# Residual transfers issued from ScalarE instead of SP, with new list rules, in a threshold-attention and MLP-mixer kernel

## Chip, cores and metric

The kernel runs on one core of one Trainium2 chip. The metric is the device time of one execution in microseconds (us). All data is float32.

## The reference

What is computed, cut to the core (8 images, 8 heads, 576 tokens, head width 64; 512 features, 256 token units, 1536 channel units):

```python
scores = scale * np.matmul(q, k.transpose(0, 1, 3, 2))
thresh = np.max(scores, axis=-1, keepdims=True) - tau
scores = np.where(scores >= thresh, scores, -1000000000.0)
attn = np.exp(scores - np.max(scores, axis=-1, keepdims=True))
attn = attn / (np.sum(attn, axis=-1, keepdims=True) + 1e-09)
x = np.matmul(attn, v)          # heads side by side: (8, 576, 512)
h = np.maximum(x.transpose(0, 2, 1) @ w_tok1, 0.0) @ w_tok2
u = x + h.transpose(0, 2, 1)
out = u + np.maximum(u @ w_ch1, 0.0) @ w_ch2
```

## The kernel before

One image is a *row* of the plan, b = 0 to 7. The attention of a row is cut into units of 128 queries by two heads' keys; two units make a *round*. A round is: scores on TensorE (L839), row maxima on VectorE (`mx`, L856), the bias on GpSimd (L862), masking (L872) and exponentials (L882) on ScalarE, the inverse sums on VectorE (L276, L277), scaling on GpSimd (L285). For b > 0 the probabilities are turned in blocks of 32 by 32 on VectorE (`turn_blocks`, tile `T`, L315) and brought to their places by four transfers a unit (`move`, tile `eT`, L327). Three units make a group of the values product (L365, L370), which fills `xT` (L374). The loads of q, k (L106) and v (L120) for later pairs of heads go out all along; `split_middle` (L341) prepares part of v on VectorE.

Beside the attention of row b runs the mixer of row b - 1: the token layers (L454, L472; their inputs are partly brought by `x_sb` transfers, L406 and L412) and, for 256 of a row's tokens, the channel layers in `make_groups`: `ch1` (L962) with a relu (`relu` on ScalarE, L967, or `relu_v` on VectorE, L970), and `ch2` (L980). The rest of the rows is put off (`spill`, L531) and done after the last attention by the class `Late`, on TensorE nearly alone.

The residual of a group: `turn_u` (L947) turns `u` on VectorE into the tile `us`, `move_u` (L954) moves it by eight transfers of 64 KB into the tile `ut`, `leave` (L994) adds `ut` to the product of `ch2` and writes the sum to `us`, and `store` (L1004) sends `us` to the output in two transfers. There is one buffer of `us` and one of `ut`, so the next group's turn waits for the stores and adds of the last group. This is done for b = 1 to 6, one group each: 48 transfers of `move_u` and 12 stores. Row 0 has two groups without `turn_u`. `Late` has its own turn and transfers (L1316, L1321), which the change leaves alone.

Each engine executes its instructions in the order in which they were listed. That order is made while the kernel is built, by the class `Scheduler`: every step is an `Op` with an engine, an estimated duration, the steps that it waits for and a rank. The scheduler keeps a clock for each engine (`pe`, `act`, `dve`, `pool`, `sp`), takes the step that can start first, and among those that can start at once the one of lowest rank. Steps that only issue transfers name them as `dmas=(count, KB, issue)`: so many issues of so many us on their queue, then the bytes at `RATE` and `LANDING` us until a step that waits for them may start. Some steps may go to either of two engines (`other`): the scheduler takes the one that can start first. Products that leave a PSUM bank use one of two banks during the attention (`banked`); the bank is free again when ScalarE or VectorE has emptied it. The scores have six banks of their own, for one round. The lines that decide a start:

```python
        def start(self, x, eng):
            t = max([d.landed or d.end + (d.lag if d.eng != eng else 0.0) for d in x.deps] + [0.0])
            if x.dmas and len(self.in_flight) == FLIGHT:
                t = max(t, self.in_flight[0])
```

While the planner's TensorE clock is under `WARM_UNTIL` = 110 us, idle time of TensorE is filled with turns of a unit matrix (`warm`).

Of the kernel before, what the change touches and what calls it, by code (L numbers as in the profile page):

```python
# [21 lines left out]
def kernel(  # L22
# [25 lines left out]
    nc = tc.nc  # L48
# [10 lines left out]
    NP = H // 2  # L59
# [486 lines left out]

    TOKEN_RANK, TOKEN_AFTER_TOKEN = 1.5, 2.5
    SLACK, SPARE = 1.0, 4.0
    FLIGHT, RATE, LANDING = 8, 214.0, 1.5
    WARM_UNTIL, WARM_GAP, WARM_TURN = 110.0, 0.6, 0.11  # L550

    class Op:
# [15 lines left out]
    class Scheduler:  # L568
# [42 lines left out]
            return t  # L611

        def start(self, x, eng):
            t = max([d.landed or d.end + (d.lag if d.eng != eng else 0.0) for d in x.deps] + [0.0])
            if x.dmas and len(self.in_flight) == FLIGHT:
                t = max(t, self.in_flight[0])
            if x.shared and eng == "dve":
                t = max(t, self.clock["pool"])
            if x.bank:
                frees = [b.free for b in self.banks if b.free is not None]  # L620
                if not frees:
                    return None
                t = max(t, min(frees))
            return max(t, self.clock[eng])
# [95 lines left out]
    sched = Scheduler()  # L720
# [3 lines left out]
    def key_op(*key):  # L724
        return keyed.get(key)

    def put(key, x):
        keyed[key] = x
        return x
# [59 lines left out]
    def make_pair(n):  # L789
        b, p = pairs[n]  # L790
        if n:
            ahead = (key_op("prep", n - 2, 0), key_op("prep", n - 2, 1))
            for lo in range(0, LOADS, 2):
                put(
                    ("load", n, lo),
                    sched.op(
                        "sp",
                        0.9,
                        lambda lo=lo: load_qk(n, (nc.sync,) * 2, range(lo, lo + 2)),
                        ahead,  # L800
                        1 if n >= NP else 0,
                        after=(key_op("load", n - 1, LOADS - 2),),
                        dmas=(2, 107, 0.58),
                    ),
                )
            slot = last_round(n - 2) if n > 1 else -1
            for which in (1, 0):
                put(
                    ("prep", n, which),
                    sched.op(  # L810
                        "dve",
                        PREP,
                        lambda which=which: prep(n, ((which, 0, S // 32),)),
                        [key_op("load", n, lo) for lo in range(0, LOADS, 2)] + [key_op("S", slot)],
                        3,
                        after=(key_op("prep", n - 1, 0),),
                    ),
                )
        free = key_op("V", last_values(n - 4)) if n >= VL else None
        if n > 1:  # L820
            put(("loadv", n), sched.op("sp", 2.0, lambda: load_v(n), (free,), 0, after=(key_op("loadv", n - 1),), dmas=(4, 70, 0.67) if n >= NP else (1, 280, 0.5)))
        put(("split", n), sched.op("dve" if n >= NP else "pool", 0.25 if n >= NP else 0.5, lambda: split_middle(n), (key_op("loadv", n), free), 2))


# [92 lines left out]
    state = {"ch2": [], "stores": [], "adds": []}  # L917
    early = {}

    def make_early(b):  # L920

        turn_main, turn_rest, move_main, move_rest = early_x(b)
        have = [key_op("X", rank_of_group(b, 0, g)) for g in range(3)]
        free = early.get(b - 1, converted)
        turns = [sched.op("dve", 1.1, lambda c=c: turn_main(c), have + free, 2) for c in range(HQ)]
        before = [x for k, x in keyed.items() if k[0] == "tok" and k[1] == b - 1 and len(k) == 3 and x.first_layer]
        moved = [sched.op("sp", 1.2, lambda i=i: move_main(i), turns + before, 0, dmas=(1, 131, 0.645)) for i in range(4)]
        last = sched.op("dve", 0.35, turn_rest, moved, 2)
        moved += [sched.op("sp", 0.6, lambda i=i: move_rest(i), [last] + before, 0, dmas=(1, 16, 0.6)) for i in range(4)]
        early[b] = moved  # L930
        xreads.setdefault(b, []).extend(turns + [last])

    def make_groups(b, halves):
        uT = xTs[b]
        reads = []
        for i in range(NOW[b]):
            s = {}
            n, nt = GR, GR // P
# [10 lines left out]
                        in_=uT[:, :, GR * i + P * m : GR * i + P * m + P].rearrange("q c (r a) -> q c a r", a=4),  # L949
                    )  # L950

            def move_u(k, s=s):
                for m in range(nt):
                    nc.sync.dma_start(  # L954
                        out=s["ut"][:, m, k, :], in_=s["us"][32 * k : 32 * k + 32, m]
                    )

# [48 lines left out]
            have = halves["20"] + (halves["21"] if i else [])  # L1006
            moved = []
            if b:
                turn = sched.op("dve", 1.2, turn_u, have + state["stores"] + state["adds"] + (converted if b == 1 else []), 5)
                reads.append(turn)  # L1010
                moved = [sched.op("sp", 1.2, lambda k=k, m=move_u: m(k), (turn,), 1, dmas=(nt, 53, 0.645)) for k in range(4)]
            relus = []
            for j in range(NJ):
                x, y = sched.banked(
# [14 lines left out]
            for t in range(nt):  # L1029
                outs = []  # L1030
                for c in range(0, NCC, wide):
                    make = sched.banked_in_two if b else sched.banked
                    x, y = make(
                        2.6 if b else 2.8,
                        lambda bank, *half, t=t, c=c, f=ch2: f(bank, t, c, *half),
                        "dve" if b else "act",
                        0.35 if b else 0.21,
                        lambda bank, t=t, c=c, f=leave: f(bank, t, c),
                        relus + moved + (converted if not b else []) + (state["stores"] if not b else []),
                        2,  # L1040
                        b,
                        1 if b else 0,
                    )
                    outs.append(y)
                    seconds.append(x)
                    if not b:
                        reads.append(x)
                    fills[b] = fills.get(b, 0.0) + x.cost * wide
                adds += outs
                stores.append(sched.op("sp", 0.35, lambda t=t, f=store: f(t), outs, 2, dmas=(1, 150, 0.35)))  # L1050
            state["ch2"], state["stores"], state["adds"] = seconds, stores, adds
        return reads

# [52 lines left out]
    def make_round(it):  # L1106
# [28 lines left out]
        for u in us:  # L1135
            b, p0, t = units[u]
            s = sched.op("pool", 1.46, lambda u=u: scale(u), (n,), 1)
            deps = [s]
            G = rank_of_group(b, p0, t // GU)
            if not b:  # L1140
                deps += [key_op("V", G - 2) if t % GU == 0 else None, key_op("T", u - 1)]
                for third in range(3):
                    x, y = sched.banked(
                        0.33,
                        lambda bank, u=u, third=third: turn(u, third, bank),
                        "act",
                        0.4,
                        lambda bank, u=u, third=third: turned(u, third, bank, nc.scalar.copy),
                        deps,
                        0,  # L1150
                        other=("dve", 0.5, lambda bank, u=u, third=third: turned(u, third, bank, nc.vector.tensor_copy)),
                    )
                    put(("turned", u, third), y)
                    deps = [x]
                put(("T", u), x)
                if t % GU == GU - 1:
                    make_group(b, p0, t // GU)
                    if t // GU == 2 and p0:
                        rows_due.append(b)
                continue  # L1160
            deps += [key_op("T", u - 1), key_op("M", u - 3)]
            put(("T", u), sched.op("dve", 1.31, lambda u=u: turn_blocks(u), deps, 4))
            put(
                ("M", u),
                sched.op(
                    "sp",
                    2.4,
                    lambda u=u: move(u),
                    (key_op("T", u), key_op("V", G - 2) if t % GU == 0 else None),
                    0,  # L1170
                    after=(key_op("M", u - 1),),
                    dmas=(4, 147, 0.645),
                ),
            )
            if t % GU == GU - 1:
                make_group(b, p0, t // GU)
                if t // GU == 2:
                    (rows_due if p0 == NP - 2 else early_due).append(b)
# [326 lines left out]
```

## Time and profile before

| | |
|---|---|
| three runs | 1259.86, 1265.16, 1265.19 us; median 1265.16 |
| profiled execution, its own time | 1261.13 us |
| its span, first to last instruction | 1259.4 us |
| busy: TensorE / VectorE / ScalarE / GpSimd | 1228.2 / 751.7 / 565.3 / 316.1 us |
| issues of `eT`, q and k loads, `ut`, v loads on SP | 504, 250, 128, 112 |

In the profile's lines PE is TensorE's matmuls, PEld its weight loads, DVE VectorE, ACT ScalarE, POOL GpSimd, SP the sync engine; a q behind the name (SPq) means the instruction queue, which issues a transfer or waits. `out<-in` are the program's tile names. "L315" is a line of the kernel. An arrow names who ended a wait. The share of the clock that TensorE was granted is 1.00 in nearly all of the span. A table by stretches gives for each its length, then busy time and number of instructions of PE, PEld, DVE, ACT and POOL, then granted clock, busy share of the transfer engines and GB/s. The mixed part, attention beside the mixer, lasts until about 892 us; what follows is `Late`.

### The profile page before, as it was taken

What the parts mean: (1) busy time and instruction counts of PE and PEld (TensorE: products, weight loads), DVE (VectorE), ACT (ScalarE), POOL (GpSimd) and SP (SyncE); (2) the same over time, 40 slices, a digit from 0 to 9 for tenths busy, and PEclk for the clock granted to TensorE, in tenths of its full rate; (3) what the DMA queues carried; (4) which work ended last, traced back from release to release, by engine and by line L of the source; (5) the groups of instructions that cost most, each with busy time, mean ns of one, the idle gap of its engine ahead of it and who ended that gap; (6) DMA issues with size and microseconds to landing.
All of it is one profiled execution on the core that took longest, in us unless ns stands there. A gap on an engine that the chain in (4) does not pass through costs nothing.

```text
span 1259.4 us, 20636 instructions
## 1 busy us (share of the span) xinstructions
PE 1228.2 (98%) x7590; PEld 989.2 (79%) x7590; DVE 751.7 (60%) x1136; ACT 565.3 (45%) x1236; POOL 316.1 (25%) x518
## 2 busy tenths in 40 slices
PE   9898999999999999999999999999999999999998
PEld 8566788797677777777777777688888888888887
DVE  6799972657667667666856766762443534444443
ACT  6998853554645664654565556530110202011120
POOL 4666641232223333233223332310001010000000
PEclk9999999999999999999999999999999999999999
DMA  9655985356777687676766866550201101021011
GB/s 165 149 135 165 242 195 118 89 121 169 163 168 161 160 169 154 171 158 151 190 145 144 191 154 153 131 152 22 59 19 65 34 26 43 17 67 26 26 34 34
DMA packets 324212, 149.17 MB, mean 118 GB/s; under 512 B 223696, under 2 KB 316880, under 8 KB 324112
## 3 DMA queue, kind: packets, MB, share of 16 engines
q1 hardware_dynamic: 322240, 147.64, 51.1%
q8 instruction: 60, 0.98, 0.3%
q10 hardware_dynamic: 1872, 0.21, 0.1%
q14 instruction: 40, 0.33, 0.1%
HBM read 47.32 MB, written 13.50 MB: 48 GB/s over the span
## 4 chain that ended last, share of the span: by engine, by line
PE 79%; DVE 6%; SPq 4%; DMA 3%; ACT 2%; issue 1%; POOL 0%; DVEq 0%; POOLq 0%
PE bank L980 12%; PE o L1326 10%; PE bank L962 10%; PE sc L839 9%; PE bank L370 8%; PE hx L1326 6%; PE bank L472 4%; PE hz L1326 4%; PE oz L1326 4%; PE hmm L1326 4%; PE bank L454 4%; PE bank L365 2%; SPq L327 2%; DVE mx L856 2%; DMA eT<-T 1%
## 5 line engine op out<-in xcount | busy, mean ns | idle before, releaser
L285 POOL TENSOR_SCALAR e<-e,rr 128x576 f32<-128x576 f32 x288 | 213.3, 758 | 294.4 <-DVE rr L277 275.8
L872 ACT ACTIVATE e<-sc,bias 128x576 f32<-128x576 f32 x288 | 194.1, 741 | 152.2 <-POOL bias L862 148.8
L882 ACT ACTIVATE e<-e,ntau 128x576 f32<-128x576 f32 x288 | 220.5, 778 | 0.3
L856 DVE TENSOR_REDUCE mx<-sc 128x2 f32<-128x1152 f32 x144 | 188.0, 1346 | 53.9 <-PE sc L839 53.6
L315 DVE STREAM_TRANSPOSE T<-e 128x1152 f32<-128x1152 f32 x126 | 169.9, 1363 | 45.8 <-POOL e L285 25.1
L980 PE MATMUL bank<-wc,g 128*128 128x256 f32 (+1 forms) x960 | 178.2, 339 | 2.6 <-ACT g L967 2.3
L962 PE MATMUL bank<-xT,wc 128*128 128x256 f32 x768 | 178.0, 385 | 2.5 <-ACT xT L374 2.0
L980 PEld LDWEIGHTS bank<-wc,g 128*128 128x128 f32 x960 | 152.4, 191 | 26.3 <-issue 4.8
L962 PEld LDWEIGHTS bank<-xT,wc 128*128 128x128 f32 x768 | 142.5, 190 | 32.0 <-issue 6.8
L839 PE MATMUL sc<-kT,qT 64*128 64x192 f32 (+1 forms) x1920 | 165.9, 334 | 0.6 <-ACT e L872 0.5
L839 PEld LDWEIGHTS sc<-kT,qT 64*128 64x128 f32 (+1 forms) x1920 | 139.0, 177 | 30.6 <-issue 17.7
L370 PE MATMUL bank<-eT,lv 128*64 128x384 f32 (+1 forms) x1024 | 135.2, 406 | 0.0
L1409 POOL TENSOR_TENSOR us<-us,ut 128x256 f32<-128x256 f32 x27 | 22.4, 844 | 385.8 <-DVE us L1247 385.8
L370 PEld LDWEIGHTS bank<-eT,lv 128*64 128x64 f32 x1024 | 74.5, 137 | 49.7 <-issue 41.9
L862 POOL TENSOR_SCALAR bias<-mx,toff 128x2 f32<-128x2 f32 x144 | 39.2, 273 | 196.8 <-DVE mx L856 189.7
L472 PE MATMUL bank<-w,a 128*128 128x192 f32 (+1 forms) x256 | 72.9, 418 | 0.4 <-DVE xT L483 0.3
L454 PE MATMUL bank<-x_sb,w 128*128 128x256 f32 x320 | 72.6, 382 | 0.3 <-DVE eT L305 0.2
L967 ACT ACTIVATE g<-bank 128x256 f32<-128x256 f32 x72 | 27.5, 382 | 99.7 <-PE bank L962 99.5
L454 PEld LDWEIGHTS bank<-x_sb,w 128*128 128x128 f32 x320 | 60.1, 190 | 10.6 <-issue 1.1
L1374 ACT ACTIVATE ga<-hmm 128x256 f32<-128x256 f32 x30 | 11.5, 383 | 117.1 <-PE hmm L1326 117.1
L1247 DVE TENSOR_TENSOR temps<-hx,temps 128x256 f32<-128x256 f32 x60 | 25.1, 418 | 56.7 <-PE hx L1326 56.6
L882 ACT ACTIVATION_READ_ACCUMULATOR e<-e,ntau 128x1 f32 x288 | 58.5, 203 | 0.0
(133 smaller groups left out, 1517.5 us busy)
## 6 DMA issues: line engine op xcount, KB each, us to landing
eT<-T SPq DMA_DIRECT2D x504, 144.0 KB, 3.0
lk<-in_k_dram SPq DMA_DIRECT2D x126, 72.0 KB, 3.0
lq<-in_q_dram SPq DMA_DIRECT2D x124, 72.0 KB, 3.2
out_dram<-us SPq DMA_DIRECT2D x32, 256.0 KB, 2.1
ut<-us SPq DMA_DIRECT2D x128, 64.0 KB, 2.1
lv<-in_v_dram SPq DMA_DIRECT2D x112, 72.0 KB, 2.6
spare<-in_moe_w_ch_dram SPq DMA_DIRECT2D x8, 512.0 KB, 3.8
extra<-in_moe_w_ch_dram SPq DMA_DIRECT2D x8, 512.0 KB, 3.9
```

What stands on the lines that cost most here:

```text
L285: nc.gpsimd.tensor_scalar(out=eh, in0=eh, scalar1=rr[:, h : h + 1], scalar2=1.0, op0=ALU.mult, op1=ALU.mult)
L315: nc.vector.transpose(out=T.rearrange("p a (c x) -> p c a x", c=NK), in_=e.rearrange("p (c a x) -> p c a x", c=NK, a=4))
L370: nc.tensor.matmul(to[r], lhsT=lv[:, j, :], rhs=e[j], start=False, stop=(c == NI - 1), skip_group_check=True)
L454: nc.tensor.matmul(to, lhsT=w1[:, t, P * m : P * m + P], rhs=x(t), start=(t == 0), stop=(t == NT - 1), skip_group_check=len(products) > 1,)
L472: nc.tensor.matmul(bank[:, n * i : n * i + n], lhsT=hidden[b][:, m, P * c : P * c + P], rhs=w2[:, m, lo : lo + n], start=(m == 0), stop=(m ...
L839: nc.tensor.matmul(sc[h][rows, f, HT * k : HT * k + HT], lhsT=qT[r, cols], rhs=kT[r, HT * f : HT * f + HT], start=True, stop=True, skip_gr ...
L856: nc.vector.tensor_reduce(out=mx[:, h], in_=sc[h][:, :, 0 : 2 * HT].rearrange("p f (k x) -> p k f x", k=2), axis=AX.XY, op=ALU.max)
L872: nc.scalar.activation(out=eh, in_=part[h], func=AF.Prelu, bias=bias[:, h], scale=SCALE, alpha=STEEP)
L882: nc.scalar.activation(out=eh, in_=eh, func=AF.Exp, bias=ntau, accum_out=rs[:, h, 0:1])
L962: nc.tensor.matmul(bank[:, 0:n], lhsT=wc1[:, j, c, :], rhs=uT[:, c, GR * i : GR * i + n], start=(c == 0), stop=(c == NCC - 1))
L980: nc.tensor.matmul(to, lhsT=s["g"][:, j, P * t : P * t + P], rhs=wc2[:, j, P * c : P * c + wide * P], start=(j == 0 and b > 0), stop=(j == ...
L1326: nc.tensor.matmul(ps, lhsT=l, rhs=r, start=start and x == 0, stop=x == len(pairs) - 1, skip_group_check=not start)
```

## The change

Five things are altered. `move_u` issues its transfers from ScalarE's queue (`nc.scalar`), as steps of the engine `act` with rank 3, and they are reckoned at 64 KB and 0.55 us per issue. The stores of rows 1 to 6 get rank -1 (2 before), 256 KB and 0.6 us. The turn of the residual is reckoned at 2.05 us (1.2 before). The issues of q and k loads, v loads, `x_sb` and `eT` are reckoned at 0.62, 0.70, 0.69 and 0.69 us (0.58, 0.67, 0.645 and 0.645 before). And a VectorE step that waits for a transfer is placed as if the transfer landed `LATE` = 2.0 us later, once the planner's TensorE clock has passed `CALM` = 200 us. What each instruction computes is the same; the planner makes another order of all of them.

```diff
--- before.py
+++ after.py
@@ -546,7 +546,7 @@
 
     TOKEN_RANK, TOKEN_AFTER_TOKEN = 1.5, 2.5
     SLACK, SPARE = 1.0, 4.0
-    FLIGHT, RATE, LANDING = 8, 214.0, 1.5
+    FLIGHT, RATE, LANDING, LATE, CALM = 8, 214.0, 1.5, 2.0, 200.0
     WARM_UNTIL, WARM_GAP, WARM_TURN = 110.0, 0.6, 0.11
 
     class Op:
@@ -611,7 +611,8 @@
             return t
 
         def start(self, x, eng):
-            t = max([d.landed or d.end + (d.lag if d.eng != eng else 0.0) for d in x.deps] + [0.0])
+            late = LATE if eng == "dve" and self.clock["pe"] > CALM else 0.0
+            t = max([d.landed + late if d.landed else d.end + (d.lag if d.eng != eng else 0.0) for d in x.deps] + [0.0])
             if x.dmas and len(self.in_flight) == FLIGHT:
                 t = max(t, self.in_flight[0])
             if x.shared and eng == "dve":
@@ -800,7 +801,7 @@
                         ahead,
                         1 if n >= NP else 0,
                         after=(key_op("load", n - 1, LOADS - 2),),
-                        dmas=(2, 107, 0.58),
+                        dmas=(2, 107, 0.62),
                     ),
                 )
             slot = last_round(n - 2) if n > 1 else -1
@@ -818,7 +819,7 @@
                 )
         free = key_op("V", last_values(n - 4)) if n >= VL else None
         if n > 1:
-            put(("loadv", n), sched.op("sp", 2.0, lambda: load_v(n), (free,), 0, after=(key_op("loadv", n - 1),), dmas=(4, 70, 0.67) if n >= NP else (1, 280, 0.5)))
+            put(("loadv", n), sched.op("sp", 2.0, lambda: load_v(n), (free,), 0, after=(key_op("loadv", n - 1),), dmas=(4, 70, 0.70) if n >= NP else (1, 280, 0.5)))
         put(("split", n), sched.op("dve" if n >= NP else "pool", 0.25 if n >= NP else 0.5, lambda: split_middle(n), (key_op("loadv", n), free), 2))
 
 
@@ -924,7 +925,7 @@
         free = early.get(b - 1, converted)
         turns = [sched.op("dve", 1.1, lambda c=c: turn_main(c), have + free, 2) for c in range(HQ)]
         before = [x for k, x in keyed.items() if k[0] == "tok" and k[1] == b - 1 and len(k) == 3 and x.first_layer]
-        moved = [sched.op("sp", 1.2, lambda i=i: move_main(i), turns + before, 0, dmas=(1, 131, 0.645)) for i in range(4)]
+        moved = [sched.op("sp", 1.2, lambda i=i: move_main(i), turns + before, 0, dmas=(1, 131, 0.69)) for i in range(4)]
         last = sched.op("dve", 0.35, turn_rest, moved, 2)
         moved += [sched.op("sp", 0.6, lambda i=i: move_rest(i), [last] + before, 0, dmas=(1, 16, 0.6)) for i in range(4)]
         early[b] = moved
@@ -949,9 +950,9 @@
                         in_=uT[:, :, GR * i + P * m : GR * i + P * m + P].rearrange("q c (r a) -> q c a r", a=4),
                     )
 
-            def move_u(k, s=s):
+            def move_u(k, eng, s=s):
                 for m in range(nt):
-                    nc.sync.dma_start(
+                    eng.dma_start(
                         out=s["ut"][:, m, k, :], in_=s["us"][32 * k : 32 * k + 32, m]
                     )
 
@@ -1006,9 +1007,9 @@
             have = halves["20"] + (halves["21"] if i else [])
             moved = []
             if b:
-                turn = sched.op("dve", 1.2, turn_u, have + state["stores"] + state["adds"] + (converted if b == 1 else []), 5)
+                turn = sched.op("dve", 2.05, turn_u, have + state["stores"] + state["adds"] + (converted if b == 1 else []), 5)
                 reads.append(turn)
-                moved = [sched.op("sp", 1.2, lambda k=k, m=move_u: m(k), (turn,), 1, dmas=(nt, 53, 0.645)) for k in range(4)]
+                moved = [sched.op("act", 1.2, lambda k=k, m=move_u: m(k, nc.scalar), (turn,), 3, dmas=(nt, 64, 0.55)) for k in range(4)]
             relus = []
             for j in range(NJ):
                 x, y = sched.banked(
@@ -1047,7 +1048,7 @@
                         reads.append(x)
                     fills[b] = fills.get(b, 0.0) + x.cost * wide
                 adds += outs
-                stores.append(sched.op("sp", 0.35, lambda t=t, f=store: f(t), outs, 2, dmas=(1, 150, 0.35)))
+                stores.append(sched.op("sp", 0.35, lambda t=t, f=store: f(t), outs, -1 if b else 2, dmas=(1, 256, 0.6)))
             state["ch2"], state["stores"], state["adds"] = seconds, stores, adds
         return reads
 
@@ -1169,7 +1170,7 @@
                     (key_op("T", u), key_op("V", G - 2) if t % GU == 0 else None),
                     0,
                     after=(key_op("M", u - 1),),
-                    dmas=(4, 147, 0.645),
+                    dmas=(4, 147, 0.69),
                 ),
             )
             if t % GU == GU - 1:
```

## The prediction

> **What bounds the kernel now.** I read the page's busy line first, then the busy times by stretch, then who ended TensorE's waits, then the time line of the queues around each of those waits.
>
> ```profile
> span 1259.4 us, 20636 instructions
> PE 1228.2 (98%) x7590; PEld 989.2 (79%) x7590; DVE 751.7 (60%) x1136; ACT 565.3 (45%) x1236; POOL 316.1 (25%) x518
> ...
> 0.00:200.00 200.00, 185.60 (x1443) 142.85 (x1443) 163.89 (x266) 158.20 (x336) 105.89 (x163) 1.00 0.76 172
> 200.00:892.10 692.10, 680.21 (x4471) 528.03 (x4472) 429.27 (x581) 352.69 (x771) 187.83 (x328) 1.00 0.64 145
> 892.10:1259.40 367.30, 362.36 (x1678) 318.34 (x1676) 158.51 (x291) 54.42 (x130) 22.42 (x27) 1.00 0.14 39
> ```
>
> The first number of a stretch is its length, the second TensorE's busy time. TensorE idles 1259.4 - 1228.2 = 31.2 us in all: 14.4 in the first 200 us (weights are converted there, and the edit of the DVE rule starts only where the planner's PE clock is past 200), 11.9 between 200 and 892 us (attention beside the mixer), 4.9 at the very end. The matmuls are the same in both kernels, and the order built from the changed one has the same number of warming turns (114) and the same order from the last values product to the end. So the change can save at most the idle time; the 11.9 us are what it aims at.
>
> ```profile
> PE bank L980 <- ACT g L967: 2.3, 2, 2.1
> PE bank L365 <- DMA x_sb<-extra: 2.2, 1, 2.2
> PE bank L962 <- ACT xT L374: 2.0, 1, 2.0
> PE bank L365 <- DMA lv<-in_v_dram: 1.3, 1, 1.3
> PE bank L978 <- DVE rr L276: 0.9, 1, 0.9
> PE bank L435 <- ACT x_sb L439: 0.7, 1, 0.7
> PE bank L365 <- DVE g L970: 0.6, 1, 0.6
> ```
>
> These are TensorE's waits from 200 to 890 us: total, times, longest. They are few and each has a place. The queue of SP (the next lines: start, duration, issues) shows what stood ahead of them.
>
> ```profile
> 323.92 3.01 SPq L954 DMA_DIRECT2D ut<-us  x4
> 327.03 5.88 SPq L327 DMA_DIRECT2D eT<-T  x8
> ...
> 520.67 0.60 SPq L1004 DMA_DIRECT2D out_dram<-us  x1
> ...
> 524.06 2.12 DVE L947 STREAM_TRANSPOSE us<-xT 128x512 f32<-128x512 f32 x2 [4.81 <-DMA out_dram<-us]
> ...
> 732.22 5.33 SPq L954 DMA_DIRECT2D ut<-us  x8
> 737.60 0.58 SPq L106 DMA_DIRECT2D lq<-in_q_dram  x1
> 738.24 0.53 SPq L106 DMA_DIRECT2D lk<-in_k_dram  x1
> 738.87 5.13 SPq L327 DMA_DIRECT2D eT<-T  x8
> 744.09 2.64 SPq L120 DMA_DIRECT2D lv<-in_v_dram  x4
> ...
> 748.60 0.36 DVE L341 TENSOR_TENSOR vl<-lv,whose 128x64 int32<-128x64 int32 x2 [3.26 <-DMA lv<-in_v_dram]
> ```
>
> SP issues back to back for 12 us after 323.92 and for 24 after 732.22, so whatever stands ahead delays all that follows. At 747.3 TensorE waited 1.3 us for lv, issued behind eight residual transfers; at 335.5 it waited 2.2 us at a values product whose last eT piece was issued at 332.3, behind four (the profile credits the last landing that it saw, x_sb). At 524.06 VectorE had stood 4.81 us at the turn of the residual, because the store that frees its buffer was issued only at 520.67; the score maxima behind it came late, and TensorE lost 2.0 us at 531.7 and 0.6 at 543.5. The 2.1 us at 760.1 is a relu of ScalarE behind late softmax work, whose maxima stood on VectorE behind transposes that waited 1.69 and 2.14 us for transfers issued up to 754.3, in the same busy stretch of SP.
>
> **The change, part by part.**
> *Residual transfers, 48 issues (6 groups x 8), from SP to ScalarE.* Taken from SP: its 48 issues last 0.602 us at the median and start 0.646 us apart (5.33 us for eight): 48 x 0.646 = 31.0 us of a queue that is busy 509 us of the 692 (821 issues). Past the others of that queue, eT, lv, lq, lk and x_sb move up by 2.6 or 5.2 us behind each place where four or eight stood. That covers the 2.2 us at 335.5 (2.6 freed), the 1.3 at 747.3 (5.2 freed) and, less surely, the 2.1 at 760.1: **-5.6 us**. The transfers themselves had slack and stay hidden: in the group issued from 732.2 the first add that reads them starts at 771.4, more than 30 us later; without that cover an add would wait their 2.1 us to landing.
>
> Added to ScalarE: the same 31.0 us, on an engine busy 352.7 of 692.1 us there. ScalarE's own issue rows (0.36 to 0.58 us, the five at the start) bound one from below, SP's row from above; I take 0.646. In the built order they stand as ten blocks of four and one of eight, so 2.6 and 5.2 us, and each first waits for VectorE's two turns (2.12 us). Directly behind ten of the eleven stands a relu (L967), behind the other a masking (L872); a PSUM bank waits for each relu, and there are two. Dearest case: the block starts when a bank is full; the bank is free 2.59 + 0.38 us later, TensorE meanwhile has one product of 8 x 0.216 = 1.73 us in the other, and loses 1.24 us; the block of eight 3.8. That is 10 x 1.24 + 3.8 = 16.2 us at most. Cheapest: nothing. The nearest row is one of ScalarE's own: four exponentials in a row (4 x 0.777 = 3.1 us) block it as long, up to 54 times in this stretch, and TensorE's waits for ScalarE there, without the two explained above, are 0.7 + 0.3 + 0.2 + 0.2 = 1.4 us, or 0.03 each. Eleven more: **+0.3 us**.
>
> *Stores first (rank -1).* No instruction added; a store is issued when the adds are done and not behind eT. It frees `us`, for which the turn waits: VectorE's 7.6 us in three waits (L947), one of which cost TensorE 2.0 + 0.6: **-2.6 us**. The eT pieces that it passes lose one issue each, 0.54 us; twelve stores, hidden by the 2.6 us blocks that left the queue.
>
> *LATE = 2.0 on VectorE's waits for transfers, dearer issues (0.69, 0.70, 0.62 in place of 0.645, 0.67, 0.58), turn at 2.05.* These only alter the list. The durations are nearer to the trace: eT issues start 0.647 us apart at the median and last 0.632 in the mean against 0.602 in the median, since 25 of 440 took over 0.8 us. The counts move: 61 relus on ScalarE and 35 on VectorE against 72 and 24; 11 x 0.42 us = 4.6 us more on VectorE, which is idle 38% of the stretch. I cost these rules at nothing by themselves, hidden behind TensorE's other products.
>
> *A new order everywhere.* Every list has places where a guess was wrong. Bounds: none, or again the 8.2 us removed. I take one stall of the usual size, **+2.0 us**; the 3.7 us of small waits stay.
>
> Sum: -5.6 - 2.6 + 0.3 + 2.0 = -5.9 us. The profiled execution took 1261.13 us (span 1259.4 and 1.7 around it), so 1255.2. The median shown, 1265.16, is 4.0 above it, the fastest run at 1259.86 below it; no trace shows what the higher ones lost. A list with less on SP should suffer less from stretched issues, so I take a third of that distance: **1256.5 us**.
>
> **Rivals.**
> 1. *New stalls for old.* The waits came from a static order against transfers of varying length, and SP still carries 773 issues. Then the 8.2 us reappear elsewhere: 1261.1 + 0.3 = 1261.4 us. For it: with the old rules already the stretches from 450 to 500 and 550 to 650 us have no TensorE idle at all, so luck counts. Against: three of the five stalls stand right behind the issues that go.
> 2. *ScalarE holds the banks (the slower side).* From 0.75 us lost per block on, 11 x 0.75 = 8.2 eats the gain; at the dearest price the time is 1261.1 - 8.2 + 16.2 + 2.0 = 1271.1 us. For it: two banks only, relus behind ten blocks, and the planner reckons 0.55 us per issue where SP's row gives 0.646. Against: ScalarE is idle half the time and the planner gives these issues its last rank.
> 3. *SP gets no relief, because the two queues issue one at a time.* Then only the stores' 2.6 us are won: 1261.1 - 2.6 + 0.3 + 2.0 = 1260.8 us. Against it, from the start of the trace:
>
> ```profile
> 0.73 0.94 SPq L106 DMA_DIRECT2D lk<-in_k_dram  x2
> ...
> 0.73 1.03 ACTq L106 DMA_DIRECT2D lk<-in_k_dram  x2
> ```
>
> Two issues on each queue in the same microsecond, none longer (0.40 to 0.58 us each) than SP's median 0.60 later, when ScalarE issues nothing. [...]
> 4. *More than the named stalls.* All idle after 200 us goes: 1261.1 - 11.9 = 1249.2 us.
>
> **How the numbers follow.** Forecast 0.43; rival 1 0.25; rival 2 0.18; rival 3 0.06; rival 4 0.08. A change of 0.5% of 1265.16 is 6.3 us, about what a measurement of this kernel can tell from none. Faster by that (below 1258.8): 0.31 of the forecast, 0.08 of rival 4, 0.02 of rival 1, together 0.41. Slower (above 1271.5): 0.13 of rival 2, 0.02 each of rivals 1 and 3, 0.17. Within: 0.42. The range leaves out the far ends of rivals 2 and 4: 1248.5 to 1268; the forecast's own is 1250 to 1261.
>
> **What would show it.** In the changed profile: the residual's issues on ScalarE's queue at about 0.65 us each, eT and lv issues without the 5 us blocks ahead; TensorE's idle from 200 us to the end of the attention near 6 us; VectorE's wait for out_dram near nothing; TensorE's waits for relus (L967) not grown. The forecast is wrong if those relu waits pass 5 us, if issues on ScalarE stretch beyond 1 us beside SP's, or if TensorE's idle time there stays near 12 us with new names.

## The result and the profile after

The changed kernel takes 1253.22 us (median of 6 runs, 1250.87 to 1255.79) against 1263.95 before (6 runs, 1259.86 to 1265.19): ratio 0.992, 95% interval 0.9901 to 0.9939, or 10.7 us less. The prediction was 1256.5. The two profiled executions, at 1261.13 and 1253.89 us, lie 7.2 us apart. The other 3.5 us of the medians' distance fit the differences in TensorE's mean granted clock, which is on record for 65 runs of the kernel before: the ten at 0.998 or more take 1260.2 us at the median, the ten at 0.993 or less 1267.4. The profiled execution of before had 0.998 where those 65 have 0.995 at the median; the profile and the runs of the changed kernel have 0.997 alike. An estimate from this is 0.003 x 1260 = 3.8 us.

The page of the changed kernel:

```profile
span 1252.1 us, 20650 instructions
## 1 busy us (share of the span) xinstructions
PE 1226.1 (98%) x7590; PEld 990.5 (79%) x7590; DVE 756.4 (60%) x1147; ACT 561.0 (45%) x1225; POOL 317.1 (25%) x518
```

Busy times by stretch, changed kernel (length, then PE, PEld, DVE, ACT, POOL busy, clock, transfers):

```profile
0.00:200.00 200.00, 186.57 (x1431) 143.22 (x1432) 163.55 (x266) 158.49 (x335) 105.92 (x163) 0.98 0.76 172
200.00:885.00 685.00, 677.34 (x4485) 529.13 (x4485) 434.50 (x592) 348.06 (x760) 188.74 (x328) 1.00 0.65 147
885.00:1252.10 367.10, 362.20 (x1677) 318.19 (x1676) 158.36 (x291) 54.45 (x130) 22.45 (x27) 1.00 0.14 39
```

The stage after the attention is as long as before; the stretch from 200 us on got shorter by the 7 us. TensorE idles 685.0 - 677.3 = 7.7 us there, against 11.9. That is 4.2 of the 7.2 us. The rest lies inside what the page counts as busy: the same 7590 matmuls are busy 1226.1 us in place of 1228.2. In the kernel before, the clock explains part of it. Behind its wait at 531.7 us TensorE was granted half the clock for 3.4 us, and like products took longer (before, TensorE's time line, then the stretch in the columns of the table above):

```profile
520.19 2.22 PE L839 MATMUL sc<-kT,qT 64*128 64x192 f32 x24
522.34 1.99 PE L962 MATMUL bank<-xT,wc 128*128 128x256 f32 x8
...
531.69 2.46 PE L962 MATMUL bank<-xT,wc 128*128 128x256 f32 x8 [2.03 <-ACT xT L374]
534.07 3.39 PE L839 MATMUL sc<-kT,qT 64*128 64x192 f32 x24
...
533.10:536.50 3.40, 3.40 (x19) 2.75 (x19) 0.77 (x4) 1.46 (x5) 1.72 (x3) 0.50 0.52 109
```

The lower two took 0.47 + 1.17 = 1.6 us longer than the upper two, so the stall at 531.7 cost 3.7 us and not 2.0. The changed kernel has no such stretch after 200 us, but one of 6.8 us from 57.4 on, which is why its first row shows 0.98. Some 1.4 us of the 7.2 stay unexplained.

TensorE's waits from 200 to 890 us, changed kernel (total us, times, longest; the four longest):

```profile
PE bank L365 <- DMA lv<-in_v_dram: 3.1, 1, 3.1
PE bank L365 <- DMA lq<-in_q_dram: 1.8, 1, 1.8
PE bank L365 <- DVE xT L483: 0.9, 1, 0.9
PE bank L365 <- DMA eT<-T: 0.8, 1, 0.8
```

All the stalls that the prediction named are gone; the two longest here are new ones, at 403.9 and 454.5 us. No relu of ScalarE stands in the list any more. From the waits of all engines in the same stretch, and from the line of the residual's issues (minimum, median and maximum in ns):

```profile
DVE vl L341 <- DMA lv<-in_v_dram: 14.1, 6, 9.5
ACT g L968 <- DMA ut<-us: 11.8, 3, 5.5
DVE T L315 <- DMA eT<-T: 7.1, 5, 1.7
```

```profile
L955 ACTq DMA_DIRECT2D ut<-us x48: 550/616/1501, 291.0 to 832.3; - x48
```

VectorE's waits for lv and eT fell to half (28.6 and 15.0 before), and its 7.6 us for the stores no longer appear. ScalarE did stand behind its own issues, 11.8 us at relus and 4.9 us at a masking, and no matmul's wait in the list above is put down to it.

The longest wait, 3.1 us, comes from the move all the same. It ends when the last eT piece has landed, at 403.7 us, and SP issued these pieces late (changed kernel: a line of SP's waits, SP's time line, TensorE's):

```profile
SPq L327 <- DMA ut<-us: 5.9, 3, 3.0
...
395.86 0.50 SPq L106 DMA_DIRECT2D lk<-in_k_dram  x1
398.77 2.50 SPq L327 DMA_DIRECT2D eT<-T  x4
...
403.88 0.87 PE L365 MATMUL bank<-eT,vl 128*64 128x384 f32 x4 [3.11 <-DMA lv<-in_v_dram]
```

SP stood 2.4 us before the eT issue, until a residual transfer that ScalarE had issued at 396.0 landed at 398.7. In this trace all 1157 transfers, of SP's queue (1104) and ScalarE's (53), report their landing on the same eight semaphores, and none of the 1149 issues that use a semaphore again starts before the transfer that used it last has landed. 33 start within 0.1 us after that landing, 13 of these behind a transfer of the other queue. The eT issue is one: it starts 0.06 us after the transfer of 396.0, which had used its semaphore, has landed. So transfers issued by ScalarE still held SP. It waited 11.0 us for residual transfers in the changed kernel from 200 to 890 us, and in no line of the kernel before. With the same list and the issues on SP (the mirror below) these eT pieces are issued from 395.80 on, and TensorE waits 0.9 us there.

### The profile page after: what moved, and what is told of

It is laid out like the page before. It is cut to its first block, busy times and chain, and to the rows that moved or that the text cites. A ratio compares the mean times of both kernels' runs of the same rounds, so it can differ in the third digit from the quotient of the medians.

```text
span 1252.1 us, 20650 instructions
## 1 busy us (share of the span) xinstructions
PE 1226.1 (98%) x7590; PEld 990.5 (79%) x7590; DVE 756.4 (60%) x1147; ACT 561.0 (45%) x1225; POOL 317.1 (25%) x518
## 4 chain that ended last, share of the span: by engine, by line
PE 87%; DVE 4%; DMA 2%; SPq 1%; issue 1%; ACT 0%; POOL 0%; DVEq 0%; POOLq 0%
PE bank L963 13%; PE bank L981 13%; PE o L1327 10%; PE sc L840 10%; PE bank L370 9%; PE hx L1327 6%; PE bank L454 5%; PE bank L472 4%; PE hz L1327 4%; PE oz L1327 4%; PE hmm L1327 4%; PE bank L365 3%; DVE mx L857 1%; SPq L327 1%; DMA lq<-in_q_dram 1%
## 5 line engine op out<-in xcount | busy, mean ns | idle before, releaser
L968 ACT ACTIVATE g<-bank 128x256 f32<-128x256 f32 x61 | 23.5, 385 | 105.9 <-PE bank L963 93.7
L454 PEld LDWEIGHTS bank<-x_sb,w 128*128 128x128 f32 x320 | 59.8, 190 | 11.8 <-ACT e L883 1.4
```

Of the source, the lines that this page charges most:

```text
L454: nc.tensor.matmul(to, lhsT=w1[:, t, P * m : P * m + P], rhs=x(t), start=(t == 0), stop=(t == NT - 1), skip_group_check=len(products) > 1,)
```

## The experiments

Each was timed against runs of the kernel before on the same chip; the ratio has its 95% interval. Differences to the changed kernel compare series whose medians of the kernel before lie between 1263.95 and 1265.38 us.

| kernel | median us | before us | ratio |
|---|---|---|---|
| changed kernel | 1253.22 | 1263.95 | 0.9920 (0.9901 to 0.9939) |
| p1: before, move alone, at its place in the list | 1257.51 | 1264.42 | 0.9953 (0.9928 to 0.9977) |
| p2: changed list, without the move | 1258.98 | 1264.42 | 0.9959 (0.9942 to 0.9976) |
| changed, LATE = 0 | 1260.29 | 1264.42 | 0.9967 (0.9948 to 0.9986) |
| changed, stores as before | 1250.22 | 1264.42 | 0.9883 (0.9854 to 0.9911) |
| before, stores first alone | 1265.74 | 1264.16 | 1.0019 (1.0006 to 1.0032) |
| before, LATE alone | 1261.54 | 1264.16 | 0.9980 (0.9961 to 0.9999) |
| changed, issues on ScalarE twice | 1275.94 | 1264.16 | 1.0098 (1.0068 to 1.0127) |
| changed, stores' rank 2 | 1251.67 | 1264.16 | 0.9914 (0.9889 to 0.9938) |
| changed, issues on ScalarE halved | 1253.34 | 1265.38 | 0.9906 (0.9884 to 0.9927) |
| changed, issue durations as before | 1258.79 | 1265.38 | 0.9949 (0.9930 to 0.9968) |
| before, all list rules, no move | 1253.76 | 1265.03 | 0.9905 (0.9888 to 0.9922) |
| changed, stores as before, LATE = 3 | 1250.71 | 1265.03 | 0.9883 (0.9868 to 0.9898) |

### The queue without the list

**Only the queue, in the list of the kernel before.**

```diff
-                    nc.sync.dma_start(
+                    nc.scalar.dma_start(
                         out=s["ut"][:, m, k, :], in_=s["us"][32 * k : 32 * k + 32, m]
```

> The list of the kernel before, unchanged in order; only the 48 issues of move_u go out from ScalarE at the place where they were listed on SP. The planner knows nothing of it, so this is the queue alone. Relief of SP (the prediction's theory): the stalls at 335.5, 747.3 and 760.1 go, 5.6 us of the 1263.95 before, so about 1258 us. New list (rival: the gain came with the new order): no gain, 1262 to 1266. ScalarE holds the banks: above 1266, with TensorE waits for relus (L967) of over 3 us.

Measured 1257.5, 6.9 us less: the relief of SP is real. TensorE's waits of this kernel, 200 to 890 us:

```profile
PE bank L962 <- ACT xT L374: 2.8, 1, 2.8
PE bank L365 <- DMA x_sb<-extra: 1.1, 1, 1.1
...
PE bank L980 <- ACT g L967: 0.9, 2, 0.6
```

The order is that of before, so places can be compared. The wait for x_sb and eT near 335 us fell from 2.2 to 1.1 us, the wait for lv at 747 us is gone, the one for the relu near 760 fell from 2.1 to 0.6. That is 3.9 of the 5.6 us priced. The clock adds to it: this trace has no stretch at half the clock between 200 and 890 us, and the nine runs have a mean clock of 0.999 where the 26 of before on that chip have 0.995. The wait behind the late store stays, as it should, since no store was moved: 2.0 before, 2.8 here, with VectorE standing 5.49 us at the turn:

```profile
522.84 2.10 DVE L947 STREAM_TRANSPOSE us<-xT 128x512 f32<-128x512 f32 x2 [5.49 <-DMA out_dram<-us]
```

**The mirror: the changed list, with the issues on SP.**

```diff
-... lambda k=k, m=move_u: m(k, nc.scalar), (turn,), 3, dmas=(nt, 64, 0.55)) ...
+... lambda k=k, m=move_u: m(k, nc.sync), (turn,), 3, dmas=(nt, 64, 0.55)) ...
```

> The list of the changed kernel, unchanged in order; only the 48 issues of move_u go out from SP at their listed place, 31 us back on that queue. Relief of SP: the 5.6 us come back, about 1259 us against 1253.2. New list: stays at 1252 to 1255.

Measured 1259.0, 5.8 us more than the changed kernel. The two agree on the move's worth with one list held fixed. This list was planned for an SP that has not these issues, though, so the mirror doesn't tell what the rules are worth without the move; the kernel for that comes below.

### The list rules

**LATE undone.**

```diff
-    FLIGHT, RATE, LANDING, LATE, CALM = 8, 214.0, 1.5, 2.0, 200.0
+    FLIGHT, RATE, LANDING, LATE, CALM = 8, 214.0, 1.5, 0.0, 200.0
```

> The changed kernel with LATE = 0: the rule on VectorE's waits for transfers alone is undone, the list is made anew. The prediction costs the rule at nothing: 1253 us, within 2. If the rule carries the gain: 1257 to 1264, and VectorE waits more for eT and lv than the 7.1 and 14.1 us of the changed kernel.

Measured 1260.3: 7.1 us of the changed kernel's gain go with a rule that had been costed at nothing. A place where it shows, VectorE's time line of this kernel, then SP's:

```profile
427.23 0.42 DVE L971 TENSOR_SCALAR g<-bank 128x256 f32<-128x256 f32 x1 [1.30 <-PE bank L963]
433.67 0.36 DVE L341 TENSOR_TENSOR vl<-lv,whose 128x64 int32<-128x64 int32 x2 [6.01 <-DMA lv<-in_v_dram]
...
436.01 1.38 DVE L315 STREAM_TRANSPOSE T<-e 128x1152 f32<-128x1152 f32 x1 [1.70 <-POOL e L285]
437.31 2.58 DVE L857 TENSOR_REDUCE mx<-sc 128x2 f32<-128x1152 f32 x2
```

```profile
429.14 2.62 SPq L120 DMA_DIRECT2D lv<-in_v_dram  x4
```

VectorE came to `vl` at 427.7 and did nothing until 433.7, when lv, issued from 429.1 on, had landed. Transposes and maxima queued behind it, and TensorE stood still for 4.3 us at 440.7, waiting for eT.

**The issue durations undone.**

```diff
-                        dmas=(2, 107, 0.62),
+                        dmas=(2, 107, 0.58),
```

and likewise 0.67 for v, 0.645 for `x_sb` and `eT`.

> The changed kernel with the issue durations of before (0.58, 0.67, 0.645, 0.645 us) for q and k, v, x_sb and eT, all else changed. The prediction costs them at nothing: 1252 to 1254.5. If the dearer issues carry part of the gain, as a place for transfers to come late: 1256 to 1260, with more of VectorE's waits for eT and lv. If they are too dear: 1249 to 1251.

Measured 1258.8, 5.6 us more; TensorE's longest wait is again one of 4.5 us for eT. VectorE's wait for lv rose only from 14.1 to 17.6 us, that for eT from 7.1 to 10.8. More of the loss lies with TensorE than was expected: with that wait it was granted half the clock for 6.8 us.

**LATE alone, in the kernel before.** The edit is that of the change's `start`, and nothing else.

> The kernel before with LATE = 2.0 past 200 us alone; issues, ranks and durations as before. Undoing it in the changed kernel cost 7 us. If the rule is worth that by itself: about 1257 us, with VectorE's waits for lv, eT and out_dram well under the 28.6, 15.0 and 7.6 us of before. If it pays only on a queue that has been relieved: 1262 to 1265.

Measured 1261.5, only 2.6 us less. VectorE's waits for lv fell from 28.6 to 14.7 us, those for the stores from 7.6 to 1.8; but TensorE has a new wait, and half the clock for 6.8 us with it:

```profile
PE bank L365 <- DMA eT<-T: 7.3, 1, 7.3
```

**All list rules, without the move.** LATE, the dearer issues and the turn at 2.05 us, the residual on SP in the planner too, stores as before:

```diff
-... [d.landed or d.end + ... ]
+... [d.landed + late if d.landed else d.end + ... ]
-                    dmas=(4, 147, 0.645),
+                    dmas=(4, 147, 0.69),
-                turn = sched.op("dve", 1.2, turn_u, ...
+                turn = sched.op("dve", 2.05, turn_u, ...
```

> The kernel before with the list rules alone: LATE = 2.0, the dearer issues and the turn at 2.05 us; the residual stays on SP, in the planner too, and the stores keep rank 2. If the rules pay by themselves (7.1 us for LATE and 5.6 for the durations were lost when each was undone): about 1252 to 1254 us. If they pay only beside the relieved queue: 1259 to 1263, as LATE alone gave 1261.5.

Measured 1253.8, 11.3 us less: as much as the whole change. TensorE's waits of this kernel, 200 to 890 us:

```profile
PE bank L365 <- DMA x_sb<-extra: 2.7, 1, 2.7
PE bank L365 <- DMA eT<-T: 2.4, 1, 2.4
```

With all of the residual's issues on SP, two long waits remain, each with 3.4 us at half the clock. The rules by themselves pay, in part for the same waits as the move: VectorE's wait for lv is 11.2 us here and 14.2 with the move alone, against 28.6 before.

### The stores

**Undone in the changed kernel, rank and numbers; then the rank alone.**

```diff
-... outs, -1 if b else 2, dmas=(1, 256, 0.6)))
+... outs, 2, dmas=(1, 150, 0.35)))
```

> The changed kernel with the stores' rank, size and duration as before (2, 150 KB, 0.35 us). The prediction gives the stores 2.6 us: about 1256 us, with VectorE's wait for out_dram back at several us. If the stores don't matter: 1252 to 1254.

> The changed kernel with the stores' rank 2 as before, but the new 256 KB and 0.6 us. Undoing rank and numbers together gave 1250.2 us. If the rank is what costs 3 us: 1250 again. If that was one list's luck: any value from 1250 to 1256.

Measured 1250.2 and 1251.7: 3.0 and 1.6 us faster than the changed kernel. The prediction had priced the stores' new rank as a gain, and undoing it as a loss. VectorE's wait for the stores did not come back without it (no such line in the waits of either), so the rank is not what removed it. The second's interval overlaps the changed kernel's almost whole, so that the rank costs anything is not shown, only that it wins nothing. These two lists also show what a block of issues on ScalarE can cost. In the first, the block of eight:

```profile
513.43 10.06 ACTq L955 DMA_DIRECT2D ut<-us  x8
523.54 0.38 ACT L968 ACTIVATE g<-bank 128x256 f32<-128x256 f32 x1 [10.39 <-DMA lk<-in_k_dram]
523.97 0.55 PE L365 MATMUL bank<-eT,vl 128*64 128x192 f32 x4 [2.88 <-ACT g L968]
```

The block takes 10.06 us, where SP's block of eight took 5.33 in the kernel before. The profile puts the relu's wait behind it, 10.39 us, down to the landing of lk, a transfer of SP's, and TensorE loses 2.9 us behind the relu, its longest wait in this kernel. With the rank alone undone, the block of eight takes 9.75 us and TensorE loses 2.5 us.

**Alone, in the kernel before** (the same edit the other way).

> The kernel before with the stores' rank -1, 256 KB and 0.6 us alone. The prediction's theory: VectorE's 7.6 us for out_dram go, and with them the 2.0 and 0.6 us behind the turn at 524, so 1261 to 1262 us against 1264.4. Rival (the rank is worth nothing, the changed kernel lost that wait through LATE): 1264, or above it where SP then stands at a store whose adds are not done, with SP's wait for the adds (L994) over the 28.9 us of before.

Measured 1265.7, a little slower (1.0006 to 1.0032). VectorE's wait at the turn did fall, from 7.6 to 2.8 us:

```profile
DVE vl L341 <- DMA lv<-in_v_dram: 23.8, 10, 8.9
DVE T L315 <- DMA eT<-T: 20.0, 12, 4.6
...
DVE us L947 <- DMA out_dram<-us: 2.8, 2, 1.8
```

But its waits for eT rose from 15.0 to 20.0, and TensorE's longest wait was 3.5 us for a values product. One wait was changed for others.

### What ScalarE pays

**The issues doubled**, each transfer in two halves, the list unchanged:

```diff
+                    for a in range(2):
-                    eng.dma_start(
-                        out=s["ut"][:, m, k, :], in_=s["us"][32 * k : 32 * k + 32, m]
+                        eng.dma_start(
+                            out=s["ut"][64 * a : 64 * a + 64, m, k, :], in_=s["us"][32 * k + 16 * a : 32 * k + 16 * a + 16, m]
```

> The list of the changed kernel, unchanged in order, with each of the 48 transfers of move_u split in two halves on ScalarE: 96 issues there, about 31 us more on that engine, blocks of 5.2 and 10.3 us. ScalarE's time is covered (the prediction's 0.03 us a block): within 1.5 us of 1253.2. ScalarE holds the banks: by its dearest row 11 blocks x (5.2 + 0.4 - 1.73 = 3.8) = 42 us more at most; over 1258 would speak for it.

Measured 1275.9, 22.7 us more than the changed kernel, 0.47 us for each further issue. From its waits, 200 to 900 us:

```profile
ACT g L969 <- DMA ut<-us: 33.2, 6, 10.5
...
PE bank L964 <- ACT g L969: 7.7, 3, 4.4
...
PE bank L365 <- ACT e L883: 5.1, 1, 5.1
```

Relus stand behind the issues for up to 10.5 us, and TensorE behind the relus and the softmax: the rival's mechanism, at twice the load. It is not the whole of the loss. SP waits 29.2 us for these transfers in place of 11.0. TensorE idles 21.3 us from 200 to 906 us, against 7.7 from 200 to 885 in the changed kernel, and it has half the clock in three stretches of 6.8 us, 16.6 us of them busy, which by estimate cost 8.3 us.

**The issues halved**: `us` and `ut` are laid out as [128, 4, 2, 128], and one transfer of 128 KB takes the place of two.

```diff
-                for m in range(nt):
-                    eng.dma_start(
-                        out=s["ut"][:, m, k, :], in_=s["us"][32 * k : 32 * k + 32, m]
-                    )
+                eng.dma_start(
+                    out=s["ut"][:, k], in_=s["us"][32 * k : 32 * k + 32]
+                )
```

> The list of the changed kernel, unchanged in order; the tiles us and ut are laid out so that two transfers of move_u become one of 128 KB: 24 issues on ScalarE in place of 48, blocks of two and four, the same bytes. Twice the issues cost 22.7 us. If the first 48 are covered (the prediction's 0.3 us in all): 1252 to 1254. If each issue costs in proportion (0.47 us): 11 us less, about 1242. In between, 1247 to 1251, the first 48 cost some 4 to 10 us. The stores read the new layout, which may cost a little.

Measured 1253.3, the same as the changed kernel. The 24 issues last 604 ns at the median, so ScalarE gave half of the time back and nothing came of it: in this list the time of 48 issues is covered, that of 96 is far beyond the cover. What SP waits for is not tested by this: it stood 3.0 us for a residual transfer at the place found above, and TensorE's longest wait is again there, 3.2 us at 403.4.

### A second list by the same rules

```diff
-    FLIGHT, RATE, LANDING, LATE, CALM = 8, 214.0, 1.5, 2.0, 200.0
+    FLIGHT, RATE, LANDING, LATE, CALM = 8, 214.0, 1.5, 3.0, 200.0
```

(on top of the stores as before)

> The fastest so far, 1250.2 us (the changed kernel with the stores as before), with LATE = 3.0 in place of 2.0: another list made by the same rules. If the rules and not one lucky list make the time: within 2.5 us of 1250. If single lists differ by as much as the parts do (3 to 7 us): 1253 to 1257.

Measured 1250.7 against 1250.2 with 2.0: another list, the same time. These two are the fastest kernels of the study, 3.0 and 2.5 us under the changed one. In all, five lists were made with LATE and the dearer issues, and take 1250.2 to 1253.8 us; the five that lack one or both take 1258.8 us and more. So one lucky list is unlikely to have made the gain.

## Why the prediction was right, and where not

The sum was right in sign and nearly in size: -5.9 us against 7.2 less between the profiled executions and 10.7 between the medians. Its terms were not all right, and one of the signs that the prediction named against itself came up: issues on ScalarE stretched beyond 1 us, 6 of 48, to 1.50 us at most. The other two did not; TensorE's idle time fell to 7.7 us (about 6 expected) and no relu wait grew.

- **SP's relief, -5.6 us.** Right where it was argued, with the list held fixed: 6.9 us less in one list, 5.8 more in the other, and the three stalls shrank at their places by 3.9 us. What the step left out is that the list rules remove the same stalls. Beside them the move is worth 1253.76 - 1250.22 = 3.5 us (list rules alone, against list rules and move with the stores as before), a difference between two series of runs. It left out too that the moved transfers still hold SP by the shared semaphores: 2.4 us at 398.7.
- **"I cost these rules at nothing by themselves."** This step failed, and it is the largest miss. The rules alone give 11.3 us; undoing LATE in the changed kernel costs 7.1, undoing the durations 5.6. The trace of before had shown VectorE waiting 28.6 us for lv, 15.0 for eT and 7.6 for the stores, each an instruction listed too early with others queued behind. I read these as SP's lateness only. They are as well the planner's, which thought the transfers earlier than they were; reckoning them later moves the waiting instructions back instead of the transfers forward. LATE alone gives 2.6 us; the dearer issues and the turn's 2.05 us were not run alone, so how the 11.3 us divide is not shown.
- **Stores first, -2.6 us.** Wrong in sign: +1.6 us alone, and the kernel is no slower without it. The wait was named rightly (VectorE at 524 us, 4.8 us), the cure was not: with the list rules and rank 2 the wait is 2.9 us without the move, and beside it gone (1.8 us with LATE = 3).
- **ScalarE's price, +0.3 us.** Right for the issues' time in this one list, shown by the halved ones, and not for the move as a whole: the wait through SP at 403.9 us is 2.2 us longer than in the mirror, and in two other lists ScalarE's block of eight costs TensorE 2.9 and 2.5 us. The next 48 issues cost 0.47 us each, clock and SP's waits included. The comparison with four exponentials gave the right size for the wrong reason, told in the last section.
- **New stalls, +2.0 us.** New ones came: 3.1, 1.8, 0.9 and 0.8 us in the changed kernel, the first by the move and not by the new order alone. They are larger than the term, but more of the old small waits went than the prediction allowed (it kept 3.7 us).
- **At most the idle time.** This bound does not hold: half the clock behind a stall lies in what counts as busy, 1.6 us behind 531.7 us in the kernel before. The step from the profiled time to the median took 1.3 of 4.0 us off for stretched issues; the runs' clocks fit that distance, and nothing here ties it to stretched issues.

So that the total came close is luck in part: a gain that was not priced and one that was wrong offset each other. Of the rivals, new stalls for old is half true. ScalarE holding the banks is hardly met in the changed kernel's list, and in two others it cost TensorE 2.9 and 2.5 us. That the two queues issue one at a time is excluded as far as p1's gain goes, though they do wait for each other's transfers (13 issues in the changed kernel start within 0.1 us after a landing of the other queue's; SP's waits for ScalarE's are 11.0 us). In the changed kernel the 15 eT issues that ran beside one of ScalarE's lasted 602 ns at the median, the 425 without one 602 as well. So the usual issue lasted no longer beside the other queue; the tail may have. Of SP's 35 issues beside one of ScalarE's 9 took over 0.8 us, of the 742 others from 200 to 892 us 31. What stretches them is not shown.

Left open: some 1.4 us of TensorE's time that the page counts as busy, how much of each gain between medians is clock and how much waiting (the list rules gain 11.3 us between medians and 5.8 between profiles, the move at its place 6.9 and 4.5), and what the stores' rank costs beside the rules. The rank's price rests on intervals that overlap.

## What to carry to other kernels

Where engines follow a list made ahead of time, measure the planner's guesses against the trace first: a few numbers that made transfers land later in the plan were worth 11.3 us, more than the 6.9 for taking 31 us of issues from the crowded queue. Price parts that could remove the same wait together, and let each be built alone and left out: here the parts' gains (6.9 and 11.3 us) don't add (14.2 together, the stores as before). The 48 issues moved to a computing engine fitted under the work queued there: halving them gave nothing back (1253.3 us against 1253.2), doubling them cost 22.7 us. Test the reserve by doubling it, and look in the trace for what the two queues still wait for in common, the eight semaphores here.

## What the runs showed of the hardware

In the changed kernel ScalarE's queue issued transfers while ScalarE still computed what was listed before them. In its time line the four issues of this block are listed behind four exponentials:

```profile
731.60 0.78 ACT L883 ACTIVATE e<-e,ntau 128x576 f32<-128x576 f32 x1
731.76 0.55 ACTq L955 DMA_DIRECT2D ut<-us  x1
...
732.36 0.62 ACTq L955 DMA_DIRECT2D ut<-us  x1
732.36 0.78 ACT L883 ACTIVATE e<-e,ntau 128x576 f32<-128x576 f32 x1
...
733.66 0.62 ACTq L955 DMA_DIRECT2D ut<-us  x1
...
733.88 0.77 ACT L883 ACTIVATE e<-e,ntau 128x576 f32<-128x576 f32 x1
```

They run from 731.76 to 734.28 us, under exponentials that last from 731.60 to 734.65: the block cost ScalarE next to nothing. In the list of the changed kernel seven of the eleven blocks stand directly behind exponentials like this one, which is the likely reason that blocks of 2.6 us did so little. In the doubled kernel the block that followed the relu at 517.5 us had no such cover, and ScalarE stood 8.5 us behind it. Single issues on ScalarE also stretched, as SP's did, to 1.50 us at most against a median of 0.62; 9 of 48 took over 0.8 us, where 1 of 48 did on SP before.

The clock that TensorE was granted fell to half (0.50) behind some of its waits, for 3.4 or 6.8 us. In the fourteen traces every such stretch between 200 and 900 us starts in a wait of 2.0 us or more or within 1.5 us behind it. All eight waits of 3.2 us or more, up to 7.3, brought one, of the eleven between 2.0 and 3.1 us five did; what decides among these is not shown. So the stall at 531.7 us in the kernel before cost 3.7 us where the list of waits has 2.0.
